# A delta-rule attention block and a multiplicative FFN on one core: output products without a drain, odd heads' scores as single products, and a new order of steps

## Chip, core and metric

The kernel runs on one core of a Trainium2 chip. The metric is device time in microseconds (us), from the start to the end of one execution of the program. The kernel before takes 555.79 us (median of three runs, 555.67 to 556.93).

## What is computed

Four batches with eight heads each run a delta rule over 768 tokens with head size 48. Its outputs, 3072 tokens of 384 features, go through an FFN that multiplies two products element by element. Everything is fp32.

```python
for t in range(S):
    kt, vt, bt = k_n[:, :, t], v[:, :, t], beta[:, :, t, None]
    y[:, :, t] = einsum('bhd,bhde->bhe', q[:, :, t], state)
    v_old = einsum('bhde,bhd->bhe', state, kt)
    state = state + bt[..., None] * einsum('bhd,bhe->bhde', kt, vt - v_old)
x = y.transpose(0, 2, 1, 3).reshape(B * S, H * D)
out = ((x @ w1) * (x @ w2) @ w3) @ w_out
```

## The kernel before

**Chunks.** Tokens are cut into 12 chunks of 64 (`NCH`). Of a chunk m, for all 32 pairs of batch and head at once, `scores` (step names `s0` to `s11` in the list, L371) makes the products K·K and K·Q, scales the first into `U` and masks the second into `PT`. `inverse` (`V0` to `V5`, L457, for two chunks at a time) inverts the triangular blocks on VectorE, in 31 dependent pairs of instructions. `corner` (`e`, L543) completes the inverses to 64 by 64. `chain` (`c`, L637) carries the state from chunk to chunk, and `outputs` (`y`, L711) makes the chunk's outputs from the state, from `X` (made by `chain`) and from `PT`.

**Small products.** Contraction and output of one head are 48 or 64 wide, so a product fills a quarter of TensorE's array: the half of partitions that its operands lie in (`feat(h % 2)`: even heads below, odd heads above) and the half that its output goes to. Products in four different quarters run beside each other. An fp32 product is two MATMUL instructions in the trace.

**What `scores` does with odd heads (L377 to L390).** For an even head one product gives K·K and K·Q side by side, 128 columns wide. For an odd head, two products of 64 columns do: K·Q is put into the other half of the partitions, crossed, as `X` and `PT` are crossed by batch pair and parity. ScalarE then copies both parities of the K·Q part into `PT` in one copy (L405), and GpSimd masks it (L407). Chunks 2 and 3 are masked by VectorE instead (L411).

**What `outputs` does.** It has two lists of products (`modes`, L722). The first holds the state's products of two of the batches and all products of `X` with `PT`, the second the state's products of the other two batches. In the second list the same half of the array writes the other PSUM bank (`region`, L717: bank `(h + z) % 2`), and a drain of TensorE stands between them (L742), with every product ordered ahead of it or behind it. Eight copies on ScalarE (L765) bring the result to `xT`. Chunk 0 has no state, so its second list is empty, though its drain is there.

**The FFN.** `w3 @ w_out` is folded into one matrix first: `fold` (`f`, L846) sums eight products per 128 rows, in the order of `kc`; product `kc` needs piece `P<kc>` of `w_out`. Weights arrive by DMA in pieces (`P`, L785), each with two instructions on ScalarE (L797, L798), two on VectorE (L800, L801) and one on GpSimd (L805). `w3` is transposed by TensorE (`t`, L836) and copied by ScalarE (L843). Pairs of chunks then go through `ab` (`a`, `b`, L862, first pair) or `eleven` (`a`, `h`, `i`, `j`, products at L988) and `o` (products at L1098), with sums on GpSimd and VectorE.

**Two product buffers.** Small products write into `two_banks()` (L155), two buffers in turn. While an `inverse` runs, it holds one of them (L471), so that each small step waits until the step ahead of it has been copied out.

**The order.** `ORDER` (L39) is a list of step names written out, made by a planner. Each name runs its generator up to the next `yield`, and `in_text_order` (L168) holds each engine to the order in which the list issued its instructions. So each engine works through its own part of the list and waits where an operand isn't there; SyncE's DMA issues stand in the same list. The name's n-th occurrence is the n-th stretch between two yields; `f1`, for example, stands in the list three times: four products, four products, and the copy to `w34`.

Of the kernel before, what the change touches and what calls it, by code (L numbers as in the profile page):

```python
# [43 lines left out]
t4 V0 V0 P5 V0 V0 P4 t10 P7 P4 t3 t3 V0 V0 P1 f1 P6 P6 t4 V0 P7 V0 V0 t10 t1 P14 P7 P4 V0 f0 V0  # L44
P6 P16 P16 V0 V0 P7 t1 s0 P19 P19 P19 P19 V0 f1 P17 k3 p2 v1 V0 V0 P14 P14 P14 V0 f2 P17 f2 f0 V0
f2 P15 v0 P20 f1 t11 f0 P17 P17 f5 V0 V0 P16 t11 P16 t8 P15 V1 V0 t8 f5 t9 V0 V0 t6 P15 V0 n0 n0
f5 V0 V0 V0 V0 t9 P20 P20 V0 t6 P22 P22 P22 f4 P23 P23 V0 f4 f4 P21 P21 P15 t7 t7 V0 s1 V0 V0 V0
V0 g1 d2 d2 P22 f3 f3 P24 P20 g1 g1 p3 g1 P26 p3 P30 e0 e0 e0 t12 t14 e1 e1 g1 f3 e0 e0 d3 d3 N1
s2 s2 s2 P23 P23 t12 e0 f6 e0 p4 s2 P24 e1 e1 t14 s2 e0 P24 s2 P25 c0 P26 f7 u2 P30 P24 c0 e1 e1
P21 P21 d3 d3 y0 y0 P26 P26 P31 t15 t13 s3 s3 s3 s3 s3 s3 t13 c0 n1 n1 P32 t15 u2 u2 u3 c0 P30 f7  # L50
e1 P25 P25 P31 P31 P27 c1 c1 u3 u3 f6 e1 c1 V1 V1 V1 y0 P31 f6 f7 P25 P27 V1 V1 V1 V1 P30 b1 c1
N1 b1 v2 P32 V1 V1 P27 V1 s1 y1 y1 b2 V1 d4 V1 V1 P28 P29 P32 b2 P27 V2 V1 V1 V1 y1 b3 V1 V1 P28
P28 b0 P32 c1 b2 b2 b3 b1 b1 b0 P29 P29 b0 P29 a03 a03 a02 V1 b0 V1 d4 V1 V1 a01 V1 P28 V1 V1 a02
V1 P35 a01 a00 a00 n2 n2 a04 a04 b7 P33 P33 a05 a05 P34 P34 a01 a07 b7 V1 b4 b5 V1 V1 V1 V1 k4
a01 a07 k5 b5 b3 g2 b4 V1 V1 P35 V1 V1 g2 c1 e2 e2 e2 e2 a06 a06 g2 e3 e3 e3 b3 g2 g2 a00 a02 a02
p4 v3 d4 d4 p5 a00 e2 P34 c2 c2 e2 P34 e2 b6 P35 P35 e2 c2 c2 e3 a03 g2 g2 P33 b6 y2 g2 P33 g2 d5
d5 p5 c2 c2 y2 a04 e3 s4 N2 e3 s4 a03 s4 b6 b6 s4 s4 s4 s4 T e3 T T d5 n3 d5 a04 e3 b4 b4 b7 s5
n3 k6 g3 u4 s5 s5 s5 s5 s5 s5 b5 b7 b5 a05 T c3 c3 a06 a05 a06 u5 V2 p6 g3 a07 a07 c3 c3 g3 S0 S0
S0 V2 g3 V2 V2 N2 oD0 y3 y3 V2 V2 W oA0 S0 S0 V2 V2 S0 S0 S0 c3 v5 n5 V2 V2 S0 S0 S0 S0 V2 v4 oB0
V2 V2 V2 xA0 V2 V2 xB0 V2 V2 oA0 S0 S0 S0 n4 oB0 xA0 d6 y3 k7 xA0 V2 n4 oC0 V2 V2 V2 a10 xB0 S0  # L60
V2 V2 xC0 G1 V2 xD0 a10 a10 V2 oC0 a10 a10 d6 xC0 xC0 xC0 xD0 V2 V2 i10 V2 h10 c3 c4 V2 V2 j10 V2
V2 V2 a10 h10 i10 a12 V2 V2 h10 W W a12 p6 V2 a12 a12 j12 e4 g3 g3 h10 c4 a12 h10 a12 h12 d6 d6
s5 i12 e4 e4 e4 i10 h12 h12 g3 g3 p7 g3 e4 e4 h12 N3 s4 h12 a11 a11 a11 s6 s6 i12 i12 e5 c4 j11
s6 c4 y4 y4 c4 e5 d7 d7 h11 c4 c5 a11 p7 e5 s6 a11 a11 h11 i11 i11 n5 c5 d7 d7 N3 a13 h11 h11 e5
W e5 s7 e5 a13 s7 s7 s7 s7 s7 s7 a13 a13 s6 s6 c5 i11 k8 u7 u6 g4 g4 g4 S1 V3 V3 c5 p8 h11 s6 g4
h13 a13 j13 a13 i13 h13 i13 i13 S1 h13 V3 h13 h13 V3 V3 y5 V3 V3 V3 V3 V3 V3 d8 V3 V3 V3 y5 oC1
oA1 S1 oD1 S1 S1 V3 V3 S1 xA1 c5 oA1 xA1 oB1 v6 y5 v7 a20 a20 V3 xA1 V3 V3 V3 d8 G2 V3 V3 xB1 n6
V3 V3 V3 V3 oB1 xB1 xC1 S1 j20 k9 V3 xD1 V3 V3 V3 V3 S1 oC1 a20 a20 p8 xC1 V3 xC1 h20 V3 xD1 xC1
V3 V3 V3 V3 a20 a20 i20 h20 a22 h20 g4 c5 g4 g4 g4 a22 V3 j22 d8 h20 h20 e6 i20 g4 a22 d8 a22 h22
a22 a22 i22 e6 V4 e6 c6 i20 h22 e6 i22 h22 n7 h22 e6 e6 a21 a21 a21 n6 c6 p9 c6 s8 i22 N4 h21 h22  # L70
i21 a21 s8 a21 s6 c6 y6 s8 s8 j21 s8 v8 a21 h21 i21 y6 d9 d9 e7 p9 e7 s8 s8 e7 e7 s7 h21 h21 i21
h21 a23 c6 c6 e7 a23 i23 a23 n8 n8 d9 e7 S2 N4 d9 a23 s9 s9 s9 s9 s9 n7 s9 k10 s9 u8 g5 a23 a23
c7 c7 h23 h23 i23 i23 c7 c7 g5 u9 h23 h23 V4 V4 V4 j23 h23 S2 g5 g5 V4 V4 V4 V4 p10 v9 V4 y7 y7
V4 V4 oA2 V4 V4 d10 V4 y7 V4 V4 S2 oD2 S2 d10 xA2 V4 S2 S2 oB2 oC2 V4 c7 xB2 V4 V4 V4 V4 oB2 xB2
xC2 xD2 p10 V4 V4 V4 oA2 V4 V4 a30 a30 G3 a30 a30 S2 S2 oC2 k11 V4 xC2 j30 s9 V4 xD2 xC2 V4 V4 V4
V4 V4 V4 xA2 xA2 xC2 g5 a30 h30 a30 i30 a32 h30 V4 V4 V4 e8 h30 i30 c7 a32 j32 h30 h30 g5 a32 a32
i32 g5 g5 d10 d10 i30 a32 a32 e8 h32 h32 i32 p11 e8 e8 a31 a31 c8 e8 s8 c8 g5 a31 j31 e8 c8 n9 c8
h32 h32 h32 y8 y8 c8 e9 e9 i31 d11 d11 h31 e9 e9 n9 a31 c8 s10 a31 p11 i32 N5 s10 s10 a31 h31 s10
s10 s10 s10 c9 c9 h31 e9 e9 d11 d11 u10 i31 i31 s11 a33 a33 S3 a33 v11 h31 h31 s11 s11 s11 s11
s11 a33 c9 i33 a33 a33 c9 h33 h33 s11 u11 i33 i33 j33 h33 h33 V5 V5 V5 V5 y9 S3 h33 V5 V5 V5 v10  # L80
n10 n10 oA3 S3 S3 V5 V5 oD3 V5 oB3 s10 y9 y9 oC3 V5 V5 S3 S3 V5 V5 V5 V5 V5 xA3 xB3 V5 V5 n11 V5
V5 oB3 V5 xB3 xD3 xC3 xC3 xD3 oA3 G4 a40 S3 S3 a40 a40 V5 oC3 N5 V5 V5 V5 xA3 a40 a40 xC3 h40 a40
h40 i40 V5 V5 V5 V5 h40 h40 V5 j40 h40 i40 V5 V5 V5 V5 a42 a42 a42 a42 i42 h42 a42 j42 xA3 V5 V5
a42 i40 h42 i42 h42 h42 a41 a41 a41 a41 h41 a41 V5 e10 e10 e10 e10 h42 n11 a41 i42 h41 i41 i41
i41 h41 e10 e11 h41 e10 c9 j41 a43 a43 a43 S4 c9 e11 e11 e11 h41 c10 c10 h43 c10 a43 e11 j43 xC3
a43 c10 a43 i43 h43 i43 i43 h43 h43 e11 h43 c10 c10 y10 y10 c11 s11 oD4 c11 c11 c11 oA4 xA4 y11
S4 S4 S4 oB4 oA4 y11 y11 S4 S4 S4 xA4 xB4 oB4 xB4 oC4 xC4 xA4 a50 xC4 S4 oC4 xC4 xD4 xD4 a50 G5
a50 h50 a50 a50 i50 a50 h50 i50 i50 h50 h50 j50 h50 a52 a52 a52 a52 i52 a52 a52 h52 a51 h52 i52
j52 h52 h52 h52 i51 a51 a51 a51 h51 i52 S5 a51 a51 h51 i51 j51 h51 h51 i51 a53 a53 a53 a53 h53
a53 a53 h53 j53 h51 h53 h53 h53 i53 i53 i53 xC4 o5 x5 o5 S5 S5 o5 o5 x5 S5 S5 S5 S5 o5 x5 x5 o5  # L90
x5 x5 x5 x5 x5 x5 S5 o5 x5 x5 x5 x5
# [4 lines left out]
def kernel(  # L96
# [14 lines left out]
    P = 128  # L111
# [21 lines left out]
    def half(z):  # L133
        return slice(C * z, C * z + C)
# [235 lines left out]

    def scores(m):  # L371
        u = Us[m % 2][:, 0 : NR * H * C].rearrange("p (r h t) -> p r h t", r=NR, h=H)
        for r in range(NR):
            KQ = KQs[m]
            ps = two_banks()
            for h in range(H):
                for z in range(2):  # L377
                    x = KQ[feat(h % 2), NR * z + r, h // 2]
                    n = 128 * (h // 2)
                    if h % 2 == 0:  # L380
                        pe.matmul(  # L381
                            ps[half(z), 0, n : n + 128], lhsT=x[:, 0, :],
                            rhs=x.rearrange("p j t -> p (j t)"), start=True, stop=True,
                        )
                    else:
                        for j in range(2):
                            pe.matmul(  # L387
                                ps[half(z ^ j), 1, n + C * j : n + C * j + C],
                                lhsT=x[:, 0, :], rhs=x[:, j, :], start=True, stop=True,
                            )  # L390
# [13 lines left out]
            if m < 2 or m > 3:  # L404
                act.copy(out=by_parity(PT), in_=psv[:, :, :, 1, :])  # L405
                yield
                pool.tensor_tensor(  # L407
                    out=PT, in0=PT, in1=smask[:].unsqueeze(1).to_broadcast([P, H, C]), op=ALU.mult
                )
            else:  # L410
                dve.tensor_tensor(  # L411
                    out=by_parity(PT), in0=psv[:, :, :, 1, :],
                    in1=smask[:].unsqueeze(1).unsqueeze(1).to_broadcast([P, NP, 2, C]),
                    op=ALU.mult,
                )
# [295 lines left out]
    def outputs(c):  # L711
        PT, St, X, KQ = PTs[c], Ss.get(c), Xs[c], KQs[c]
        py = two_banks()
        pyv = py[:].rearrange("p x (b a t) -> p x b a t", b=B, a=2)

        def region(h, z, r):
            return pyv[feat(h // NP), (h + z) % 2, NR * z + r, h % NP // 2, :]  # L717
# [5 lines left out]
        for mode, todo in enumerate(modes):  # L723
# [8 lines left out]
            for r in range(NR if mode == 0 else 0):  # L732
                for a in range(NP):
                    for h in (a, NP + a):
                        for z in range(2):
                            x = half((z + h) % 2)
                            todo.append((h, z, r, X[x, r, h, :], PT[x, r, h, :]))
        part = [(h // NP, (h + z) % 2) for todo in modes for h, z, *_ in todo]
        issued, n = ([], []), 0
        for mode, todo in enumerate(modes):  # L740
            if mode:
                drain = pe.drain().ins  # L742
# [7 lines left out]
        for i in issued[0]:  # L750
            in_order(i, drain)
# [7 lines left out]
        for z in range(2):  # L759
# [85 lines left out]

    def fold(jc):  # L846
        ps = bank([P, CW])
        for kc in range(KF):
            pe.matmul(  # L849
                ps[:, 0:DM], lhsT=w3Ts[jc, kc // 4][:, kc % 4 * P : kc % 4 * P + P],  # L850
                rhs=wo[:, kc], start=(kc == 0), stop=(kc == KF - 1),
            )
            if kc == KF // 2 - 1:
                yield
# [433 lines left out]
```

## Time and profile before

| | |
|---|---|
| median of three runs | 555.79 us |
| profiled execution, its own time | 556.14 us |
| its span, first to last instruction | 554.1 us |
| TensorE, first product to last product's end | 4.6 to 550.2 us |
| TensorE's instructions (two for a product) | 8540 |
| ScalarE busy | 188.1 us |
| VectorE busy | 388.0 us |

The 2.0 us between span and time lie ahead of the first and behind the last instruction. The page cuts the span into 40 slices of 13.9 us and gives the busy tenths of each engine. A group's line gives its count, the busy time, the mean ns of one, and the idle time of the engine ahead of it with what ended that. The chain of work follows back from the last instruction to what released it. PE is TensorE, DVE VectorE, ACT ScalarE and POOL GpSimd.

### The profile page before, as it was taken

The page shows a single profiled execution, that of the slowest core. Times are in us where ns is not written, and L with a number is a line of the kernel's source. Part 1 is how long each engine was busy: PE and PEld are TensorE (multiplying, and loading weights), DVE is VectorE, ACT ScalarE, POOL GpSimd, SP SyncE. Part 2 cuts the span into 40 slices and gives each one's busy share as a digit, 9 for nine tenths or more (in the row PEclk, how much of TensorE's full clock was granted, in tenths as well). Part 3 has the DMA queues.
Part 4 walks back from the last instruction along what each step waited for, and adds up shares of the span by engine and source line. Part 5 has one row for each costly group of instructions (what it writes and reads, how often), then busy time and mean ns, then how long its engine had stood idle before and what let it go on. Part 6 is the DMA issues. An engine that isn't in the chain of part 4 may idle for free.

```text
span 554.1 us, 19883 instructions
## 1 busy us (share of the span) xinstructions
PE 520.0 (94%) x8540; PEld 446.7 (81%) x8540; DVE 388.0 (70%) x850; ACT 188.1 (34%) x393; POOL 256.6 (46%) x278
## 2 busy tenths in 40 slices
PE   2486998999999999999999999999999999999997
PEld 2473566688778988889988889988899888998897
DVE  3889999899876878659977579859587654123332
ACT  3688388954542112332022430123221121300000
POOL 8576473723659970455443355510482212342141
PEclk9998999999999999999999999999999999999999
DMA  8986987579457345455553564253411220020001
GB/s 247 197 200 211 161 224 126 138 157 151 63 80 128 76 110 82 60 100 89 99 108 64 82 120 76 92 83 46 106 31 44 63 50 2 10 66 1 0 1 57
DMA packets 197687, 52.64 MB, mean 95 GB/s; under 512 B 185344, under 2 KB 191488, under 8 KB 197600
## 3 DMA queue, kind: packets, MB, share of 16 engines
q1 hardware_dynamic: 193408, 50.59, 44.8%
q10 hardware_dynamic: 4192, 0.79, 1.0%
q8 instruction: 67, 1.10, 0.8%
q14 instruction: 20, 0.16, 0.1%
HBM read 41.25 MB, written 8.91 MB: 91 GB/s over the span
## 4 chain that ended last, share of the span: by engine, by line
PE 74%; DVE 4%; ACT 1%; issue 1%; DVEq 0%
PE ps_f L988 35%; PE ps_f L1098 19%; PE ps_w L645 5%; PE ps_w L744 4%; PE ps_f L869 4%; PE ps_w L574 2%; PE ps_w L381 1%; PE ps_w L387 1%; DVE ps_w L487 1%; DVE tb L482 1%; ACT TT L547 1%; PE ps_w L1098 1%; DVE KQ L337 0%; DVE ab L885 0%; DVE Ub L501 0%
## 5 line engine op out<-in xcount | busy, mean ns | idle before, releaser
L996 DVE TENSOR_TENSOR ab<-ab,ps_f 128x512 f32<-128x512 f32 x80 | 54.5, 682 | 58.5 <-PE ps_f L988 57.8
L1069 POOL TENSOR_TENSOR ab<-ab 128x512 f32<-128x512 f32 (+1 forms) x56 | 61.4, 1118 | 41.5 <-PE ps_f L1098 24.4
L988 PE MATMUL ps_f<-xT,w1s 128*128 128x256 f32 x320 | 78.5, 382 | 0.0
L1035 POOL TENSOR_TENSOR ab<-ab,late 128x512 f32<-128x512 f32 x19 | 24.2, 1272 | 107.6 <-DVE ab L996 106.1
L988 PEld LDWEIGHTS ps_f<-xT,w1s 128*128 128x128 f32 x320 | 59.9, 190 | 7.9
L1098 PE MATMUL ps_f<-w,ab 128*128 128x192 f32 x376 | 65.5, 328 | 0.0
L1098 PEld LDWEIGHTS ps_f<-w,ab 128*128 128x128 f32 x376 | 61.3, 190 | 1.3 <-issue 0.5
L849 PE MATMUL ps_f<-w2s,w3T 128*128 128x384 f32 x128 | 45.3, 505 | 4.9 <-POOL w2s L805 4.9
L407 POOL TENSOR_TENSOR PT<-PT,smask 128x512 f32<-128x512 f32 x20 | 25.6, 1283 | 50.9 <-ACT PT L405 50.9
L1098 PE MATMUL ps_f<-room,ab 128*128 128x192 f32 x272 | 47.2, 328 | 0.0
L498 DVE TENSOR_TENSOR ps_w<-ps_w,tb 128x31 f32<-128x31 f32 (+15 forms) x124 | 43.3, 349 | 4.2
L765 ACT COPY xT<-ps_w 48x256 f32<-48x256 f32 x96 | 30.5, 366 | 44.5 <-PE ps_w L744 44.0
L1098 PEld LDWEIGHTS ps_f<-room,ab 128*128 128x128 f32 x272 | 44.3, 190 | 0.6 <-issue 0.3
L493 DVE TENSOR_TENSOR tb<-ps_w,Ub 128x31 f32<-128x31 f32 (+15 forms) x124 | 41.9, 338 | 3.6 <-ACT ps_w L473 0.3
L1004 ACT COPY ab<-ps_f 128x512 f32<-128x512 f32 x20 | 11.7, 585 | 95.1 <-PE ps_f L988 95.0
L988 PE MATMUL ps_f<-xT,room 128*128 128x256 f32 x160 | 41.1, 384 | 0.0
L849 PEld LDWEIGHTS ps_f<-w2s,w3T 128*128 128x128 f32 x128 | 24.0, 194 | 20.4 <-POOL w2s L805 5.5
L988 PE MATMUL ps_f<-xT,w2s 128*128 128x256 f32 x160 | 40.1, 381 | 0.0
L988 PE MATMUL ps_f<-x_room,w2s 128*128 128x256 f32 x160 | 38.9, 386 | 0.0
L988 PEld LDWEIGHTS ps_f<-x_room,w2s 128*128 128x128 f32 x160 | 29.5, 190 | 5.2 <-DVE late L996 1.0
L988 PEld LDWEIGHTS ps_f<-xT,w2s 128*128 128x128 f32 x160 | 30.1, 190 | 4.1
L988 PEld LDWEIGHTS ps_f<-xT,room 128*128 128x128 f32 x160 | 29.6, 190 | 4.7 <-DVE osb L1128 0.6
(146 smaller groups left out, 1005.5 us busy)
## 6 DMA issues: line engine op xcount, KB each, us to landing
raw<-in_moe_w_dram SPq DMA_DIRECT2D x16, 512.0 KB, 5.6
vtok<-in_v_dram SPq DMA_DIRECT2D x24, 192.0 KB, 4.5
raw<-in_moe_w_dram SPq DMA_DIRECT2D x24, 192.0 KB, 4.6
out_dram<-osb SPq DMA_DIRECT2D x46, 96.0 KB, 1.7
ktok<-in_k_dram SPq DMA_DIRECT2D x44, 96.0 KB, 3.4
raw<-in_moe_w_out_dram SPq DMA_DIRECT2D x8, 384.0 KB, 4.2
perm<-in_k_dram SPq DMA_DIRECT2D x40, 64.0 KB, 3.0
perm<-in_q_dram SPq DMA_DIRECT2D x32, 64.0 KB, 2.6
```

The lines of the kernel that those rows point to most:

```text
L407: pool.tensor_tensor(out=PT, in0=PT, in1=smask[:].unsqueeze(1).to_broadcast([P, H, C]), op=ALU.mult)
L493: dve.tensor_tensor(out=tv, in0=V[:, 0 : s + 1, s : s + 1].to_broadcast([P, s + 1, n]), in1=U[:, s, s + 1 : BS].unsqueeze(1).to_broadcast( ...
L498: dve.tensor_tensor(out=o, in0=o, in1=tv, op=ALU.subtract)
L645: pe.matmul(out(ps, r, h, z), lhsT=lhs(r, h, z), rhs=rhs(r, h, z), start=True, stop=True,)
L744: i = pe.matmul(region(h, z, r), lhsT=lhs, rhs=rhs, start=part[n] not in part[:n], stop=part[n] not in part[n + 1 :],)
L765: act.copy(out=xT[f, p:NP:2, b : b + NR, cc, :].rearrange("p a r t -> p r a t"), in_=pyv[f, z, b : b + NR],)
L849: pe.matmul(ps[:, 0:DM], lhsT=w3Ts[jc, kc // 4][:, kc % 4 * P : kc % 4 * P + P], rhs=wo[:, kc], start=(kc == 0), stop=(kc == KF - 1),)
L988: pe.matmul(acc[name][:, n * i : n * i + n], lhsT=ws[b][:, P * i : P * i + P], rhs=xs[x], start=new and k == 0 and i == 0, stop=k == len(t ...
L996: dve.tensor_tensor(out=o_, in0=x, in1=acc[name], op=ALU.add)
L1035: eng.tensor_tensor(out=Z1, in0=Z1, in1=late, op=ALU.mult)
L1069: pool.tensor_tensor(out=o_, in0=x_, in1=y_, op=op)
L1098: pe.matmul(ps[b][:, b, :], lhsT=block(u, HF * f + i, z)[:, P * b : P * b + P], rhs=ws_[w][:, i], start=first and i == 0 and (b == 0 or n ...
```

## The change

Four things change.

- `SWAPPED` names nine chunks: 1 and 4 to 11. For them `scores` makes one product of 128 columns for an odd head too, uncrossed, and ScalarE sorts the K·Q part into `PT` by four copies of 64 partitions in place of one copy of 128.
- For the same chunks `outputs` begins with a step of its own: two ScalarE copies of half of `X` to the other half of the partitions, into `Xc`, a buffer of the tag "o" that squares and stores use too. All products then write bank `h % 2`, the lists are one, and there is no drain. Four copies of 512 columns in place of eight of 256 bring the result to `xT`. The drain of chunk 0 goes as well, since it is now issued only where a second list has products.
- `fold` takes `kc` in the order 0, 3, 2, 5, 1, 4, 6, 7 in the first fold and 0, 3, 2, 1, 5, 4, 6, 7 in the others.
- `ORDER` is the same for its first 135 names, and new from there: 1467 names against 1458, the nine more being the first step of the nine `y`.

```diff
+    SWAPPED = (1, *range(4, NCH))
     def scores(m):
...
-                    if h % 2 == 0:
+                    if h % 2 == 0 or m in SWAPPED:
                         pe.matmul(
-                            ps[half(z), 0, n : n + 128], lhsT=x[:, 0, :],
+                            ps[half(z), h % 2, n : n + 128], lhsT=x[:, 0, :],
...
             if m < 2 or m > 3:
-                act.copy(out=by_parity(PT), in_=psv[:, :, :, 1, :])
+                if m in SWAPPED:
+                    for z in range(2):
+                        for e in range(2):
+                            act.copy(
+                                out=PT[half(e), NP * z : NP * z + NP, :],
+                                in_=psv[half(z), :, e, 1, :],
+                            )
+                else:
+                    act.copy(out=by_parity(PT), in_=psv[:, :, :, 1, :])
...
     def outputs(c):
+        swapped = c in SWAPPED
+        if swapped:
+            Xc = in_turn(ffn, [P, NR * NP, D], "o", 2, "Xc")
+            for e in range(2):
+                act.copy(
+                    out=Xc[half(e)].rearrange("p (r a) d -> p r a d", r=NR),
+                    in_=X[half(1 - e)].rearrange("p r (a e) d -> p r a e d", e=2)[:, :, :, e],
+                )
+            yield
...
-            return pyv[feat(h // NP), (h + z) % 2, NR * z + r, h % NP // 2, :]
+            return pyv[feat(h // NP), (h if swapped else h + z) % 2, NR * z + r, h % NP // 2, :]
...
-        for mode, todo in enumerate(modes):
+        for mode in range(2):
+            todo = modes[0 if swapped else mode]
...
+            for r in range(NR if mode == 0 and swapped else 0):
+                for a in range(0, NP, 2):
+                    for z in range(2):
+                        for h in (a, a + 1, NP + a, NP + a + 1):
+                            x = half(h % 2)
+                            todo.append((
+                                h, z, r, Xc[x, NP * r + h // 2, :] if z else X[x, r, h, :],
+                                PT[x, r, NP * z + h // 2, :],
+                            ))
...
-            if mode:
+            if mode and todo:
                 drain = pe.drain().ins
...
+        for e in range(2):
+            f = feat(e)
+            for p in range(2 if swapped else 0):
+                act.copy(
+                    out=xT[f, p:NP:2, :, cc, :].rearrange("p a b t -> p b a t"), in_=pyv[f, p]
+                )
...
     def fold(jc):
+        turn = (0, 3, 2, 5, 1, 4, 6, 7) if first else (0, 3, 2, 1, 5, 4, 6, 7)
+        for i, kc in enumerate(turn):
```

The part of the list in which the two first differ, before and after:

```
P1 f1 P6 P6 t4 V0 P7 V0 V0 t10 t1 P14 P7 P4 V0 f0 V0 P6 P16 P16 V0 V0 P7 t1 s0 P19 ...
P1 P4 P6 f1 t10 P6 V0 P7 P14 V0 V0 V0 P6 P7 V0 t4 V0 V0 s0 P7 V1 V0 V0 P14 f2 P16 P16 f1 f2 f2 P19 P17 P17 t1 f1 P19 P14 V0 f0 t1 f0 ...
```

## Prediction

> **What bounds the kernel now.** I read the page's busy times and slices first.
>
> ```profile
> PE 520.0 (94%) x8540; PEld 446.7 (81%) x8540; DVE 388.0 (70%) x850; ACT 188.1 (34%) x393; POOL 256.6 (46%) x278
> ...
> PE   2486998999999999999999999999999999999997
> ...
> DVE  3889999899876878659977579859587654123332
> ACT  3688388954542112332022430123221121300000
> ```
>
> TensorE is full from the fourth slice on, so from about 46 us the time is its work plus what it waits. VectorE is full too from slice 2 to 10, to some 140 us, and ScalarE nearly so in slices 5 to 8: there another engine can set TensorE's waits. The chain of waits between 318 and 330 us shows one `outputs`:
>
> ```profile
> 325.51 1.49 PE ps_w L744 x96
> 327.00 0.12 issue
> 327.12 0.66 PE ps_w L744 x32
> ```
>
> The first list takes 1.49 us for 96 instructions, then TensorE waits for nothing but its own drain. The stretches table around the first fold, with columns for busy us and count of PE, PEld, DVE, ACT, POOL, then the granted clock, DMA share and GB/s:
>
> ```profile
> 40.00:44.00 4.00, 1.15 (x7) 0.53 (x5) 3.55 (x6) 3.97 (x7) 2.52 (x3) 1.00 0.66 225
> 44.00:46.00 2.00, 0.00 (x0) 0.00 (x0) 1.68 (x4) 1.92 (x5) 1.98 (x2) 1.00 0.01 4
> 46.00:48.00 2.00, 1.97 (x4) 1.09 (x5) 1.86 (x8) 2.00 (x6) 0.86 (x1) 0.58 0.92 295
> 48.00:50.00 2.00, 2.00 (x7) 1.00 (x6) 1.86 (x6) 1.67 (x4) 1.06 (x2) 0.57 0.73 231
> 50.00:54.00 4.00, 4.00 (x16) 2.48 (x15) 3.69 (x11) 2.89 (x6) 2.27 (x3) 1.00 0.86 290
> ```
>
> ScalarE has no gap from 40 to 48. TensorE idles 4.9 us there, and then works to 49.7 at half clock. Last, the groups by form, for ScalarE's copies:
>
> ```profile
> L765 ACT COPY xT<-ps_w 48x256 f32<-48x256 f32 x96 | 30.5, 366 | 44.5 <-PE ps_w L744 44.0
> ...
> L405 ACT COPY PT<-ps_w 128x512 f32<-128x512 f32 x20 | 11.7, 585 | 25.5 <-DVE U L393 25.5
> ```
>
> Adding the start-to-start times of TensorE's steps undisturbed (their medians by kind and neighbour) from 39.9 us on gives 487.6 us. The last step starts 507.6 us after that point, so 19.9 us are waits: 6.8 around the first fold, some 5.5 in gaps of 0.1 that come everywhere, 6 in single waits between 82 and 161 us, and under 1.5 behind that.
>
> **What TensorE saves.** *Drains.* In the timeline the groups of four X products start 0.0557 us apart. From the last one (326.76) to the first of the second list (327.12) it is 0.354, and the next group stands 0.088 behind. Against 0.0557 each that is 0.33 lost, nine times: 3.0 us. That joining the lists costs no gap itself is seen in the first list, where the products change from state to X at the usual 0.036. Chunk 0's drain: its step takes 1.26 where 16 groups at 0.0557 make 0.9 and the change to large products some 0.1; 0.25. *Odd heads.* Groups of 64 columns start 0.0583 apart, those of 128 columns 0.109 (timeline at 391 us). A half chunk has 16 of the former in step, 0.933; afterwards 8 of the latter, 0.872. 0.06 times 18 half chunks is 1.1. *Islands.* In the timeline's starts, eight FFN products take 1.73 ahead of their like and 1.82 ahead of a small step, and a small step takes about 0.12 longer ahead of a large one. Runs of small steps between large ones are 58 in the list before and 62 in the new: 4 times 0.21, +0.85. **Sum on TensorE: -3.0 - 0.25 - 1.1 + 0.85 = -3.5 us**; adding step by step through the new list gives -3.1. I take -3.3.
>
> The Trainium skill (TensorE: Matmul & The Clock Gate, section "Wait — 56ns, not 53.3ns?") has start-to-start never below about 25 ns, so that instructions and not columns would be the price here; an estimate by it is 7.2 us for the 288 that odd heads no longer issue. The trace speaks against it: four instructions go in 55.7 ns, 13.9 each.
>
> **What ScalarE gets.** Copies of 256 columns stand 0.32 apart in a row of eight, so four take 1.33 us where one took 0.585: +0.75 for each half chunk. `Xc` is two copies of 384 columns; L1133 (480 ns) is the nearest row, 0.9 for both, and bounds are 0.37 and 1.1 each (copies with strided input, L444). Four evacuations of 512 columns take 2.2 against 2.6. In all some +18 us on an engine that is 34% busy: hidden, except in three places.
>
> *First place, s1's first copy.* It lies in the unchanged part of the list, at 40.70, inside the stretch without a gap. All that follows on ScalarE moves by 0.75: the pieces' conversions, the copies of `t3` and `t4`, and the columns for V0, which VectorE waited for at 44.3. So VectorE's dense stretch starts **0.75** late.
>
> *Second place, the first folds.* Before, TensorE waits for piece P1 until 46.03 and then has work without end. In the new list the first half's fourth product (5) needs `t3`'s copy (46.95 before, now 47.7). The next step, f2, needs `t4`'s copy, which now stands behind P6, t10 and P7: 49.7, plus 0.75 is 50.45. TensorE has then done only f1's half, which before was done at 49.76. Then f0's second half needs t1's copy, which is listed behind two results, P17 and P19: about 1.1 of wait. The three folds end at 64.95 against 63.1. The half clock comes behind that: before, it lasted from 46.3 to 49.7 (products 0.64 apart, not 0.32), costing 1.7. Now TensorE idles 5 us, works for 1 and waits again, so the half clock begins when f2 does, and costs that 1.7 with nothing done beneath it.
>
> *Third place, the product buffers*, below.
>
> **The front, to 167 us.** I followed the new list by hand with the durations of the trace. VectorE's work up to the transposition in e2 (its `corner` for chunk 2, ending 141.83) is 92.3 us from P6's conversion on before, 93.9 in the new list: +1.6. It also waits more: s3's products stand behind y0's eight copies, and c1's state behind P31 and six pairs of V1. In all e2's second product, at 144.55 before, comes at about 148, with TensorE's own work ahead of it the same to 0.1: +3.4. From there to s5's second half the new list waits 0.4 less: **+3.0**. Of the half clock's 1.7, about **+0.8** reaches this point, since VectorE sets the pace for much of it.
>
> **Behind 167 us.** While an inverse holds one buffer, a step must wait until the step ahead has left the other. For a half chunk's scores that took, from TensorE's next start, 0.22 + 0.05 + 0.70 + 0.03 + 0.61 = 1.6 us (s5 at 164 to 166.6); with four copies 2.35. The list's work between the two is 1.84 before c5, 1.99 before s6's second half, 1.84 before c7: 0.35 to 0.5 short each. e4's second product (0.96 of cover against 1.45) and y8 (1.82 against 2.2, with `Xc` in the way) are short too, as is s7 before and after. Sum 2.7 against 1.2 of waits before: +1.5, if ScalarE is free at once and the list's cover is as I sum it; below it 0. I take **+0.7**.
>
> **Sum:** -3.3 + 3.0 + 0.8 + 0.7 = +1.2 against the profiled execution's 556.14, so 557.3. That execution lies 0.35 above the median of the runs, so I forecast **557.0 us**: a change within 0.3%, about what a measurement of this kernel can tell from no change (1.7 us, 554.1 to 557.5).
>
> **Rivals.** *The front keeps up (faster).* The waits to 167 us come out as before, because the new list puts other work into them than I saw; then -3.3 and at most +0.5 behind: 553.0 to 553.5. For it: TensorE is 94% busy, and its saved work is certain. Against: VectorE's 1.6 more ahead of e2 and the 0.75 at s1. 0.23.
>
> *Instructions are the price of scores (faster).* A half chunk has 48 of them in 0.933 us, 19.4 ns each; 288 fewer would be 5.6 us, not 1.1: 552.5. Against: a group with twice the columns takes 0.109 against 0.058. 0.02. (This is the rule of the skill's page above.)
>
> *The four copies hold the buffer (slower).* Where they come to a ScalarE that has just begun another copy (0.585, or `Xc`'s 0.9), each of six close places loses 0.6 more: +3.6, and 560.6. It decides from the point where the list's cover is under 2.35 us. For it: six places are. Against: ScalarE is 10 to 40% busy there. With half of it 558.8. The clock belongs here as well: half clock for twice as long costs another 1.7, of which 0.8 arrives. The Trainium skill (TensorE: Matmul & The Clock Gate, section "What's actually happening") says that the clock is raised after one free-running window of 3.4 us that was busy. The trace's 3.4 us at half clock agree, and by that rule a start in the middle of a window stays cold for up to two. 0.32.
>
> *The drain goes, the stall stays (slower).* TensorE may stop between the lists for another reason; then 3.2 come back: 560.2. Against: no gap where state products meet X products. 0.03.
>
> **Numbers.** Forecast 0.40, faster 0.25, slower 0.35. The range, 553.0 to 560.5, takes in both main rivals but for their ends.
>
> **What would show it.** Right: no gap inside L744's 128 instructions, 1.8 us for them; L381 with all scores of nine chunks; TensorE's second fold starting near 50.4 with the clock at half until 53 or later; e2's second product near 148; 0.3 to 0.5 us waits ahead of c5 and c7 for L405's successors. Wrong: e2 at 145 or before (then 553), or TensorE waits of over 1 us behind scores late in the span (then 560).

## The result, and the profile after

The changed kernel takes **563.99 us** (median of four runs, 561.0 to 565.64) against 555.73 us: a ratio of 1.0124 (95% interval 1.0087 to 1.0161). Forecast were 557.0 us, with 553.0 to 560.5 as the range. So the change is slower, by some 7 us by this ratio, and outside the range. The profiled execution took 563.97 us; its last product ends at 558.4 us, against 550.2 us before: **8.2 us** later.

The page's busy times, slices, granted clock and the queue of TensorE's code, after:

```profile
PE 523.7 (93%) x8252; PEld 445.7 (79%) x8252; DVE 391.3 (70%) x850; ACT 208.8 (37%) x429; POOL 257.1 (46%) x278
...
PE   2485998899999999999999999999999999999997
...
DVE  3888897899975897767995669967587655123422
ACT  3688377783655201553113441114521113400000
...
PEclk9996998999999999999999999999999999999999
...
q8 instruction: 65, 1.06, 0.8%
```

TensorE has 288 instructions fewer and is busy 3.7 us longer: a slower clock (0.6 in slice 4, 0.8 before) and products that take longer where they now stand. The chain of waits around one `outputs`, and the stretches table around the first fold:

```profile
334.31 1.51 PE ps_f L1032 x7
335.82 1.94 PE ps_w L777 x128
```

```profile
40.00:44.00 4.00, 3.28 (x18) 2.14 (x17) 2.68 (x6) 3.91 (x11) 1.58 (x2) 1.00 0.74 260
44.00:46.00 2.00, 0.00 (x0) 0.00 (x0) 1.88 (x2) 1.97 (x3) 1.86 (x3) 1.00 0.01 4
46.00:48.00 2.00, 0.00 (x0) 0.00 (x0) 1.65 (x4) 1.92 (x5) 1.75 (x2) 0.63 0.15 37
48.00:50.00 2.00, 0.88 (x2) 0.50 (x2) 1.86 (x7) 1.98 (x5) 0.96 (x1) 0.50 0.69 256
50.00:54.00 4.00, 3.00 (x6) 1.36 (x5) 3.69 (x12) 3.93 (x8) 2.31 (x3) 0.50 0.88 292
54.00:58.00 4.00, 4.00 (x10) 2.21 (x9) 3.73 (x10) 0.00 (x0) 2.05 (x3) 0.65 0.76 181
```

The drain is gone: 128 instructions in one piece, where there were 96, a gap and 32. In the second table TensorE (first pair) idles from 43.3 to 49.1, and the granted clock (third from the end) is at half from 46.5 to 56.8 us, three times as long as before. The groups that changed, ScalarE's copies and the fold:

```profile
L893 PE MATMUL ps_f<-w2s,w3T 128*128 128x384 f32 x128 | 48.5, 530 | 7.7 <-ACT w3T L882 7.7
...
L412 ACT COPY PT<-ps_w 64x256 f32<-64x256 f32 x72 | 26.3, 365 | 20.6 <-DVE U L397 19.9
```

**Where the 8.2 us are, by kind**, from 39.5 us on: gap inside the first fold +0.95 (5.83 against 4.88), waits for nothing that the profile shows ("issue") +1.0 (1.5 against 0.5), other waits and small gaps +2.1, half clock +3.1 (half of TensorE's busy time in it: 4.85 against 1.71), TensorE's work at full clock +1.0. **By place**: chunk 5's first scores, step `s5`, begin at 172.6 against 163.1 (+9.5), and from there to the last product it takes 385.8 against 387.1 (-1.3).

### The profile page after: what moved, and what is told of

It is laid out like the page before. It is cut to its first block, busy times and chain, and to the rows that moved or that the text cites. A ratio compares the mean times of both kernels' runs of the same rounds, so it can differ in the third digit from the quotient of the medians.

```text
span 562.2 us, 19362 instructions
## 1 busy us (share of the span) xinstructions
PE 523.7 (93%) x8252; PEld 445.7 (79%) x8252; DVE 391.3 (70%) x850; ACT 208.8 (37%) x429; POOL 257.1 (46%) x278
## 4 chain that ended last, share of the span: by engine, by line
PE 81%; ACT 9%; DMA 4%; DVE 3%; issue 1%; SPq 0%; DVEq 0%; ACTq 0%
PE ps_f L1032 35%; PE ps_f L1142 19%; PE ps_f L893 6%; PE ps_w L657 6%; PE ps_f L913 5%; PE ps_w L777 4%; DMA raw<-in_moe_w_dram 4%; PE ps_w L586 2%; PE ps_w L385 2%; ACT PT L412 1%; ACT columns L456 1%; ACT raw L837 1%; ACT KQ L360 1%; ACT w3T L882 1%; DMA ktok<-in_k_dram 1%
## 5 line engine op out<-in xcount | busy, mean ns | idle before, releaser
L893 PE MATMUL ps_f<-w2s,w3T 128*128 128x384 f32 x128 | 48.5, 530 | 7.7 <-ACT w3T L882 7.7
L510 DVE TENSOR_TENSOR ps_w<-ps_w,tb 128x31 f32<-128x31 f32 (+15 forms) x124 | 43.3, 350 | 4.3
L893 PEld LDWEIGHTS ps_f<-w2s,w3T 128*128 128x128 f32 x128 | 25.4, 207 | 25.8 <-issue 9.8
L412 ACT COPY PT<-ps_w 64x256 f32<-64x256 f32 x72 | 26.3, 365 | 20.6 <-DVE U L397 19.9
L844 POOL TENSOR_TENSOR w<-w,raw 128x512 uint32<-128x512 uint32 x16 | 21.4, 1343 | 27.2 <-DVE w L840 13.7
```

Source lines behind the costliest of these rows:

```text
L412: act.copy(out=PT[half(e), NP * z : NP * z + NP, :], in_=psv[half(z), :, e, 1, :],)
L510: dve.tensor_tensor(out=o, in0=o, in1=tv, op=ALU.subtract)
L893: pe.matmul(ps[:, 0:DM], lhsT=w3Ts[jc, kc // 4][:, kc % 4 * P : kc % 4 * P + P], rhs=wo[:, kc], start=(i == 0), stop=(i == KF - 1),)
```

## The experiments

Theory at first: the new list's front (to 165 us) costs, by late first folds and the clock behind them, and the code saves. Rival: ScalarE's added copies cost. Ratios are to runs of the kernel before on the same chip; its medians there were 556.5 to 557.6. "Drained" below means as before, with the drain; in two expectations "chunk 4's scores" at 163 to 172 us are `s5`'s, chunk 5's by the count from zero. A list joined from two takes so many steps of the one, then all that are left in the order of the other.

**1. List and code by themselves.** The old list with the new code, the new list with the old code, the new list only behind 155 us, and the change without its chunk 1:

```diff
 code_old_list:  new code, old list, yN once more ahead of the first yN of nine chunks
 list_alone:     old code, new list less the first yN of nine chunks
 old_front:
-    SWAPPED = (1, *range(4, NCH))
+    SWAPPED = range(4, NCH)
-        turn = (0, 3, 2, 5, 1, 4, 6, 7) if first else (0, 3, 2, 1, 5, 4, 6, 7)
+        turn = range(KF)        # and the list joined: 508 steps of before, then after
 chunk1_drained: new code and list
-    SWAPPED = (1, *range(4, NCH))
+    SWAPPED = range(4, NCH)
```

> All edits of the code, with the list of before; the nine added steps (one in each of chunks 1 and 4 to 11) stand right ahead of those chunks' outputs. Theory (the list's first 510 steps cost the time, the code alone saves some): 551.5 to 554.5 us, since from the first step of chunk 4's scores to the last product the changed kernel took 391.0 us against 394.9. Rival (the code costs: 72 copies of 365 ns on ScalarE, 20 us more of its time, come late for the products): 558 us or more.

> The list of after without its nine added steps, the code as before. Theory (the list's front costs): 563 to 568 us, the 12 us by which chunk 4's scores start later in the changed kernel (167.5 against 155.3 us) kept, and nothing saved behind. Rival (the code costs): 554 to 558 us.

> The list of before up to the first step of chunk 4's scores (508 steps), then what is left in the order of the list of after; chunks 4 to 11 without a drain, chunk 1 and the parts of a fold as before. Theory (front costs, the part behind saves): 551 to 553 us. Rival (the list behind that point, or the copies of chunks 4 to 11, cost): 557 us or more.

> The changed kernel with chunk 1 left as before: two copies of scores instead of four at 41 us on ScalarE, its outputs with the drain, its added step left out. If ScalarE's longer stretch at 41.5 to 43.0 us is what makes the transposes' copies, and so the first folds, late: 557 to 561 us. If the order of the front alone does it: 562 to 565 us.

Measured: `code_old_list` 1.0351 (1.0307 to 1.0395); `list_alone` 564.4 us, 1.0133 (1.0111 to 1.0154); `old_front` 559.8, 1.0060 (1.0036 to 1.0085); `chunk1_drained` 565.3, 1.0152 (1.0132 to 1.0173). The list alone makes the whole loss, as expected. But the theory's other half fell: with the old list, or with the old front, the code does not save, it loses. `code_old_list` (577.7 us, where each added step stands right ahead of its products) is the slowest of all; its loss was not taken apart. And chunk 1's four copies at 41 us are not what makes the folds late.

**2. The code with its step in better places, and the clock behind the first fold.**

```diff
 code_early:       old list, SWAPPED = range(4, NCH), folds as before; first yN right behind the fourth cN
 after_filled / before_filled: in the first fold, ahead of its fourth (second) product
+                for _ in range(24):     # 20 in before_filled
+                    pe.matmul(ps[:, DM : DM + P], lhsT=ident[:], rhs=ident[:], start=True, stop=True)
 after_fold_plain: new code and list
-        turn = (0, 3, 2, 5, 1, 4, 6, 7) if first else (0, 3, 2, 1, 5, 4, 6, 7)
+        turn = range(KF)
```

> The list of before with the code of chunks 4 to 11 changed (no drain, single products, one shape of copies); the added step of each of them stands right behind the step that writes X. Chunk 1 and the folds as before. Theory (the code saves, the list's places cost): 551.5 to 554 us, since 128 products of an outputs step took 2.01 us without and 2.34 us with a drain (8 x 0.33 = 2.6 us) and the front is untouched. Rival (the code's copies cost wherever they stand, as in the 577.7 us of the old list with the step right ahead of its products): 558 us or more.

> The changed kernel with 24 products of the identity by itself (128 by 128, into 128 columns of the first fold's bank that nothing reads) ahead of the first fold's fourth product, where TensorE stood idle from 43.28 to 49.1 us. They compute nothing that is used. Theory (the idle time there brings 10.2 us of half clock, and the part of that which is busy costs half its length): 559 to 562 us, some 3 us less than 564. Rival (the front is bound by the conversions, a full clock only waits longer): 563 to 566 us.

> The kernel before with 20 such products ahead of the first fold's second product, where TensorE stood idle from 41.15 to 46.03 us. They compute nothing that is used. Theory (clock): 554 to 555 us, 1.7 us less, half of the one window of 3.4 us at half clock behind that gap. Rival (conversions bound): 556 us, no change.

> The changed kernel with a fold's parts in the order 0 to 7, as before. If the new order (0, 3, 2, 5 first) is what makes the first fold wait longer (its fourth product waits for the second transposed copy, written by ScalarE at 48.4 us): 560 to 562 us. If the list's order on ScalarE alone does it: 563 to 566 us, since the second half of the first fold needs the same copy.

Measured: `code_early` 563.7, 1.0110 (1.0058 to 1.0163); `after_filled` 569.4, 1.0213 (1.0165 to 1.0260); `before_filled` 567.7, 1.0170 (1.0120 to 1.0220); `after_fold_plain` 563.3, 1.0096 (1.0065 to 1.0126). In the filled kernels the added products stand inside the first fold's sum, in its bank, so that fold's sum is not the reference's.

`before_filled` turned the study. It removed the gap and the half clock behind it, and was 1.9 us *ahead* of the kernel before at chunk 3's first scores (94.8 us); then it lost almost 14 us in a part in which nothing was edited. Its waits from 90 us on, those put down to "issue" (line waited at, us in total, times, longest):

```profile
PE ps_w L645 <- issue: 5.1, 4, 2.1
PE ps_w L574 <- issue: 2.5, 2, 1.3
...
PE ps_f L1001 <- issue: 0.7, 1, 0.7
PE ps_w L381 <- issue: 0.7, 1, 0.7
```

The kernel before has 0.5 us of such waits in all. One of those of `before_filled` in the timeline, inside a single `corner` step, put down to no operand:

```profile
232.59 0.71 PE L574 MATMUL ps_w<-T,U 33*33 33x32 f32 x60
234.60 0.30 PE L574 MATMUL ps_w<-T,U 33*33 33x32 f32 x4 [1.30 <-issue]
```

Counting TensorE's MATMUL rows from the start, the nine stalls of this kernel lie at rows 1236, 2125, 2380, 3649, 3776, 6062, 6316, 6824 and 7967: within two rows of multiples of 127 from each other. The queue that the page calls q8 instruction brings packets of 16 KB; the kernel before has 67 of them for its 8540 rows, 127 rows each. And each stall ends 1.28 to 1.60 us after such a packet has landed (here one landed at 233.17). **TensorE waits for its own code.** An edit that adds or takes rows moves every later block's end, into or out of stretches of short products. Over 19 traces, all but that of `code_old_list`, there are 47 breaks of more than 0.6 us put down to "issue" from 60 us on. Of these, 46 lie at rows 86 to 94 modulo 127, and each of the 46 ends 1.2 to 1.7 us after a packet's landing. The other (`chunk1_drained`, row 1422) stands where the kernel before waits for a converted piece of weights.

**3. A whole block of rows as the control, and where in the front the loss arises.**

```diff
 before_block / after_block: ahead of the first fold
+            for i in range(64):
+                z = half(i % 2)
+                pe.matmul(ps[z, 0:C], lhsT=ident[z, z], rhs=ident[z, z], start=True, stop=True)
 old_to_e0: new code, folds as before; 264 steps of before, then after
 old_to_c2: the same with 480 steps
```

> The kernel before with 64 products of the identity (64 by 64, two halves in turn) ahead of the first fold; they compute nothing that is used. 64 products are 128 rows of the trace, and the stalls of the filled runs lay 127 rows apart or a multiple of it, each 1.2 to 1.6 us behind the landing of a 16 KB packet of the instruction queue. Theory (TensorE's code comes in blocks of 127 rows; a shift by one whole block leaves every later place as it was, 40 rows moved them all): 554 to 556.5 us against the 567.7 of 40 rows. Rival (added products cost, whatever their number): 562 us or more.

> The changed kernel with the same 64 products ahead of its first fold; they compute nothing that is used. Theory (half clock of 10.2 us behind the first fold's gap, and code in blocks of 127 rows): 560 to 562.5 us, up to 3 us less than 564, as far as the products fill the gap. Rival (added products cost): 568 us or more.

> The changed code (all nine chunks) with the list of before for its first 264 steps (to 82 us) and the rest in the order of the list of after; a fold's parts in the order 0 to 7. If what the changed kernel loses comes with the folds' places (chunk 0's corner at 87.2 instead of 82.4 us): 557 to 560 us. If it comes later in the front: 562 to 565 us.

> The same with the list of before for 480 steps (to chunk 2's chain, some 146 us); chunk 1's added step right behind the step that writes X. Theory (the list's front costs, code and list behind save 3.9 us): 552.5 to 556 us. Rival (code and list must be planned together: what stands in the old order stalls with the new code): 560 us or more.

Measured: `before_block` 556.9, 1.0005 (0.9980 to 1.0029); `after_block` 564.0, 1.0133 (1.0100 to 1.0167); `old_to_e0` 562.5, 1.0106 (1.0066 to 1.0146); `old_to_c2` 561.0, 1.0071 (1.0037 to 1.0104). 128 rows cost nothing where 40 rows cost 10 us (567.7 against 557.3): the theory of blocks holds against "added products cost". The two fillings differ in size and place too, so `after_shift32` in experiment 4 is the cleaner test. The waits of `before_block` from 90 us on:

```profile
PE ps_f L876 <- POOL PT L407: 1.6, 1, 1.6
PE ps_w L574 <- ACT late L599: 0.5, 1, 0.5
...
PE ps_w L744 <- issue: 0.2, 1, 0.2
```

`after_block` has no gap in the first fold, and its third fold ends at 65.0 instead of 68.8, but chunk 5's scores begin at 172.6 as in the changed kernel. In `old_to_e0`, which keeps the old folds and their list altogether, `s5` begins at 172.3. So the folds' loss, real as it is, does not show at `s5`. That it costs nothing is not shown: `after_block` has one window more at half clock between 60 and 110 us than the changed kernel (two against one).

**4. The front of the list, and block places kept or moved on purpose.**

```diff
 list_front:        old code; 513 steps of after, then before
 chunk1_padded:     chunk1_drained, and the loop of experiment 3 with range(48)
 code_early_padded: code_early, and the loop with range(18)
 best:              old_front's code, 463 steps of before, then after, and the loop with range(48)
 after_shift32:     new code and list, and the loop with range(16)
 best_padded_later: best, the loop ahead of the first product of part b6, at some 150 us
```

> The code of before; the list of after (without the nine added steps) up to the first step of chunk 4's scores, then what is left in the order of the list of before. If the list's front makes the loss: 561.5 to 565 us, near the 564.4 of the whole list. If it is made evenly along the list, by more changes between large and small products: 557 to 560 us.

> The changed kernel with chunk 1 as before, and 48 products of the identity (96 rows, nothing that is used) ahead of the first fold, so that with the 32 rows more of chunk 1 every later row stands 128 rows on, one block. If chunk 1's copies on ScalarE cost (its added step, four copies for two): 558 to 561 us. If they don't, and the 565.3 without the pad was chunk 1's saving against stalls at blocks: 562 to 564 us.

> The kernel of 563.7 us (list of before, code of chunks 4 to 11 changed) with 18 products of the identity (36 rows, nothing that is used) ahead of the first fold. Blocks of 127 rows that pass in under 3.2 us by the rows' own times: seven, 7.1 us short in all, without the pad, and 3.9 us short with it. Theory (code blocks): 558 to 561 us. Rival (no such rule): 563 to 566 us.

> Code of chunks 4 to 11 changed, folds and chunk 1 as before; the list of before for 463 steps (to 140 us), then the order of the list of after; 48 products of the identity (96 rows, nothing that is used) ahead of the first fold, by which blocks of 127 rows are 1.8 us short in all. Theory (front of the list costs, code saves where its blocks are supplied): 552 to 555.5 us. Rival (the list behind 140 us costs as much as the code saves): 556 to 559 us.

> The changed kernel with 16 products of the identity (32 rows, nothing that is used) ahead of the first fold: every later row stands where it stands in the kernel with chunk 1 drained (565.3 us). If the places of code blocks make the front late: chunk 4's first scores at 168 to 169.5 us as there, and behind them 390 us instead of 385.8, 563 to 566 us in all. If chunk 1's copies on ScalarE do: chunk 4 at 172 us or later, and 566 us or more in all, since the places behind are the bad ones.

> As best, but the 96 rows stand at 150 us (48 products of the identity ahead of the first products of part b6, nothing that is used), so that the first 463 steps keep the block places of the kernel before and the rest those of the changed kernel. They cost up to 3 us themselves (31 ns a row). Theory (code saves where its blocks are supplied): 552 to 555 us, from 163.5 to the second step of chunk 4's scores, 386 behind it, 3 for the rows, and 5.6 outside TensorE's span of products. Rival (list and code lose elsewhere): 557 us or more.

Measured: `list_front` 560.6, 1.0054 (1.0035 to 1.0073); `chunk1_padded` 564.2, 1.0119 (1.0103 to 1.0135); `code_early_padded` 563.6, 1.0110 (1.0094 to 1.0125); `best` 560.5, 1.0057 (1.0037 to 1.0078); `after_shift32` 565.7, 1.0143 (1.0119 to 1.0168); `best_padded_later` 560.0, 1.0039 (1.0014 to 1.0065).

The traces, in us: begin of `s5`, and from there to the end of the last product.

| kernel | front: list, code, rows ahead of it | s5 begins | behind it |
|---|---|---|---|
| before | old, old | 163.1 | 387.1 |
| before_block | old, old, +128 | 164.3 | 387.1 |
| list_front | new, old | 166.2 | 386.8 |
| list_alone | new, old | 168.8 | 390.8 |
| chunk1_drained | new, chunk 1 old | 168.1 | 390.5 |
| after_shift32 | new, new, rows as chunk1_drained | 168.3 | 391.2 |
| after | new, new, 32 rows fewer | 172.6 | 385.8 |
| after_block | as after, +128 | 172.6 | 386.9 |
| after_fold_plain | as after, folds old | 172.5 | 386.2 |
| chunk1_padded | chunk 1 old, rows as after_block | 172.2 | 386.2 |

`after_shift32` is the clearest. 16 products that compute nothing put the rows where they stand with chunk 1 drained, and the front becomes that kernel's, 4.3 us shorter, while the part behind becomes that kernel's too, 5.4 us longer. Even the stalls are the same ones. Around chunk 5's first `chain` products, in the timelines of `chunk1_drained`, of `after_shift32`, and of the changed kernel:

```profile
235.54 0.90 PE L657 MATMUL ps_w<-S,KQ 48*64 48x48 f32 x45
237.45 0.55 PE L657 MATMUL ps_w<-S,KQ 48*64 48x48 f32 x19 [1.00 <-issue]
```

```profile
236.28 0.90 PE L657 MATMUL ps_w<-S,KQ 48*64 48x48 f32 x44
239.01 0.55 PE L657 MATMUL ps_w<-S,KQ 48*64 48x48 f32 x19 [1.84 <-issue]
```

```profile
239.98 0.64 PE L657 MATMUL ps_w<-S,KQ 48*64 48x48 f32 x31
240.55 1.13 PE L1032 MATMUL ps_f<-xT,room 128*128 128x256 f32 x4
```

The first two stop ahead of the last 19 rows, at row 3645 of the count; the third runs through. `chunk1_padded` makes the same point from the other side: with chunk 1's old code but the changed kernel's places its front is 172.2. So chunk 1's copies cost the front nothing that can be seen, and the places of its 32 rows cost 4.3.

**Misses.** `code_early_padded` missed: by my sum over blocks it should have lost 3.2 us of stalls, and it has 5.6 us of "issue" against 4.8. That sum called a block short below 3.2 us, which was a guess; in the 46 breaks TensorE goes on 2.2 to 3.1 us after the packet's transfer began. Where a stall can be follows from the count of rows; how long it is, and which of the dense blocks stalls, does not follow from the time in which a block's rows run. `best` and `best_padded_later` missed as well. The latter has the stalls away (0.6 us of "issue") and 386.6 us behind `s5`, as expected, but `s5` begins at 170.4 where 163.5 was expected: 3.6 us late already at chunk 1's last `chain` products (121.2 against 117.6, behind 10.2 us of half clock and a wait of 1.75 us that the profile puts down to a DMA), and as much again to `s5`. That second part stays open. Other forecasts missed too: `after_filled` and `before_filled` by the whole loss, `after_block` (564.0, not 560 to 562.5), `old_front`, `code_early` and `old_to_c2`, where the code was to save. `list_front` (560.6) fell between its two. No version here beats the kernel before.

## Why the prediction was wrong

Its sum was -3.3 (TensorE) + 3.0 (front) + 0.8 (half clock) + 0.7 (buffers). The runs take it apart like this: list's front +3.1 (`list_front`), places of 32 rows in the front +4.3 (`after` against `after_shift32`), behind `s5` -1.3, and some 2 us between `list_front` and the other kernels with that front. The trace of `list_front` is the fastest of its six executions, 2.0 us below their median, so those 2 us may be no more than that execution's luck.

- **Drains: right.** The step's 128 instructions take 2.01 us and took 2.34: 0.33 less, as summed (the 1.8 us given for them in one piece was too low). The rival in which the stall stays without the drain is out.
- **Odd heads: right ahead of large steps, smaller elsewhere; that the total agrees is luck.** From `list_alone` to the changed kernel, the rows of the scores of chunks 4 to 11 take 16.4 us instead of 17.7, -1.3 (forecast -1.1 for nine chunks). But 1.0 of it lies in three half chunks that pause inside in `list_alone` (1.4 to 1.5 us each, for a reason not found). Of the other 13, six ahead of a large step save 0.07 each (1.08 to 1.01), as forecast, four ahead of a small one 0.02 (0.95 to 0.92), and three wait for copies behind their rows. Instructions are not the price: that rival is out.
- **Islands, +0.85: the first step that failed, by its size.** The old code in the new list works 4.8 us longer on TensorE than in the old list (502.2 against 497.4 from 39.5 us on, busy time less half of that at half clock). Some 1.6 of it is large steps that now stand beside small ones (eight instructions, the prediction's "eight FFN products", take 1.92 us between small steps and 1.73 between their like), some 3 lies in the small steps. What makes those longer was not found, except for the three half chunks above. I counted runs of small steps, 58 and 62, and priced four more. Behind `s5` the list alone costs 4.0 (390.8 against 386.8 in `list_front`), and the code gives 5.0 back, of which 8 x 0.33 are drains, 1.3 scores, and 0.9 a wait that went (row 4916 of `list_alone`, 90 modulo 127; the profile puts it down to VectorE).
- **The list's front, +3.0: right in size for the list, not shown in its reason.** I followed it by hand with the old durations, and `list_front` is what that describes: e2's second product stands at 147.7, forecast near 148, `s5` begins 3.1 later, and the ratio of its runs (1.0054) is 3.0 us. But VectorE was to set that. Up to 148 us `list_front` waits 0.2 us for VectorE and, outside the folds, 1.9 and 1.1 us for ScalarE's work on weights (L796, L855) and 1.3 us of "issue"; that product follows a large step without a wait. So the size is in part luck. In the changed kernel it stands at 154.2.
- **First folds and clock.** The second fold begins at 51.7 (forecast 50.45) and the half clock lasts 10.2 us, three windows, not the one that a cost of 1.7 means (TensorE is busy for 0.24 and 0.71 of the first two). Even the rival "half clock for twice as long" was too small. It costs 3.3 us there instead of 1.7, and yet `s5` is as late where the gap is filled and that half clock gone (`after_block`, 172.6), and with the old folds (`old_to_e0`, 172.3).
- **ScalarE's copies: near.** Four take 1.49 us at `s1` (forecast 1.33), and ScalarE works 20.7 us more (forecast 18); by `after_shift32` against `list_alone` (168.3, 168.8) they cost the front nothing.
- **Product buffers, +0.7: right in kind.** From the wait ahead of `s5` on, the changed kernel waits 1.7 us, against 0.6 from `s5` on before: +1.1. Of the 1.7, 1.4 are put down to L405's successor:

```profile
PE ps_w L385 <- ACT PT L412: 0.8, 1, 0.8
PE ps_w L657 <- ACT PT L412: 0.6, 2, 0.3
```

- **What was missing altogether: the supply of code.** 288 rows fewer, and the first 32 of them at 37 us, move the end of each block behind. In the front of the changed kernel one end falls into chunk 0's `corner`:

```profile
91.27 0.26 PE L586 MATMUL ps_w<-TT,late 64*33 64x32 f32 x1 [1.50 <-issue]
```

With the 0.31 of wait ahead of it, this break leaves the window of 3.4 us around it only 0.58 busy, and the next one runs at half clock (1.5 us more). That is 3.0 us. All five traces with the changed kernel's places have a break in this step (0.4 to 2.3 us) and a window at half clock behind it. The front of `after_shift32` has two breaks instead, of 1.4 and 1.0 us, in windows 0.60 and 0.72 busy, behind which the clock stays up; against 0.58, the 0.60 is a close call. How the 4.3 us between the two come together with the waits behind was not taken apart. No term of the sum, and none of the rivals, had this.

The Trainium skill (Runtime: NRT & Kernel Launch, section "Instruction fetch mechanics") says that an engine's code is refilled in blocks of 16 KiB, 256 instructions, and calls the cost of passing a block's end "mostly hidden". The traces agree on the size (16 KB, 127 rows of MATMUL with as many weight loads) and not on the cost: 0.7 to 3.1 us in each of the 46 breaks, and waits for "issue" of 0.5 us in all before the change and 11 us in `after_filled`.

## What to carry to other kernels

When an engine runs thousands of short instructions without loops, an edit's price includes where it puts the ends of its code blocks: look for waits put down to "issue" inside a step, count instructions between them, and repeat the edit with idle instructions added up to a whole block before judging it. Separate a new order from new code by running each alone; a hand-followed order can be right in size, as here, and the total still wrong by what neither part shows by itself. A wait taken away from a full engine pays its own length (0.33 us here), while a change of order that puts small products between large ones more often can cost as much again.

## What the runs showed of the hardware

**The clock's windows.** The half clock came in stretches of 3413 ns on one grid per execution, whose phase differs from run to run. Over 18 traces with such stretches, from 39 us on: after a window at full clock in which TensorE was under 0.45 busy the next was at half each time (22 of 22), between 0.45 and 0.65 in 9 of 30, at 0.65 or more never. At half clock a window of 0.72 or less kept it (8 of 8), one of 0.83 or more ended it each time. So a wait of 1.5 to 2 us costs its length, or up to 1.7 us more (half a window), by where it falls in the grid. Two executions of the same front, `list_front` and `list_alone`, reached `s5` at 166.2 and 168.8, with no such stretch behind 39.9 us and with two; `list_alone` also has a break of 0.9 us at row 1615 that `list_front`, with the same rows, has not.
